# Scores of both head halves of four attention tiles in one group of matmuls, in a list-scheduled attention, GLU and tanh kernel

## The chip, the cores and the metric

The kernel runs on one core of a Trainium2 chip. The metric is the device time of one execution in microseconds (us). TensorE (PE in the views) multiplies, VectorE (DVE), ScalarE (ACT) and GpSimd (POOL) work on elements, and SyncE (SP) issues the transfers (DMAs). A matmul writes into one of eight banks of the accumulator memory PSUM, from which DVE and ACT read.

## The reference, cut to what matters

```python
# q, k, v: 2 batches x 8 heads x 768 tokens x 64; nb = 24 blocks of 32 tokens
k_sum = k.reshape(B, H, nb, 32, D).max(axis=3)
v_sum = v.reshape(B, H, nb, 32, D).mean(axis=3)
scores_l = q @ k^T / 8, only where |i - j| < 16, else -1e9
scores_s = q @ k_sum^T / 8 + log(32)
a = softmax(concat(scores_l, scores_s))
x = a @ concat(v, v_sum)                      # 1536 tokens x 512
xn = x / sqrt(mean(x * x) + 1e-6) * rms_g
x = (silu(xn @ w_gate) * (xn @ w_val)) @ w_out   # d_ff 1536
h = x @ w_in                                   # d_ff 2048
out = (h - tanh(h)) @ w_out2
```

## The kernel before

The attention is cut into 12 tiles of 128 tokens, and each tile into two halves of four heads: 24 units. `one_unit` (line 730) registers the operations of a unit. It loads queries, keys and values into a buffer `u` (line 741, by SP, one of three buffers), and for the later tiles POOL copies the summary keys into it (line 754). Then come eight instructions on PE, four matmuls of two passes each, that form the scores (line 786). They contract over 64 rows and go in turn to two PSUM banks, one for the even heads and one for the odd. DVE adds the mask and takes the maxima out of these banks (line 800, four), ACT takes the exponentials (line 814, four), PE transposes them (lines 834 and 839), ACT copies the transposes, PE multiplies with the values (line 877, and line 888 for the rest), and DVE and ACT scale. After both halves a tile is squared and summed (line 933), POOL takes a power (lines 923 and 924), and four transposes put the tile in columns (line 928).

Between the units stand products of the GLU. `step` takes one part of 128 columns of the hidden layer and a group of tokens. It forms the first products (lines 1046 to 1048, three matmuls for each product, since the numbers are split in a high and a low part) in a bank of the pool "mid", and later the second products in banks of the pool "bank". PSUM's eight banks are shared out as six of "bank", of which the running sums of the second products hold four and attention gets two, and two of "mid", which the first products use in turn. In the listings banks of the first pool are named bank_78 to bank_83 and those of the second mid_84 and mid_85. While the tiles 4 to 11 are worked through, PE alternates between units and steps. That stretch runs from 51 to 193 us. After it come the remaining GLU products, the wide stage and the second layer. Parts of the second layer's weights are made ahead by `make_out`: two loads (line 1607), three operations on DVE (lines 1614 and 1615), and a store (line 1617, `kd`).

The order on each engine is drawn up before the program is written. `Plan.order` is a greedy list scheduler: each operation has an engine, a duration, operations that it follows, slots (buffers or banks) that it occupies, and a latest start `late`. Of the ready operations an engine takes the one with the earliest latest start. `NUDGES` is a table whose entries shift the latest starts of a stretch of operations by random amounts, so that another table draws another order. `emit` writes the program in that order. Each engine then works through its list strictly in order, SP with its transfers too.

Of the kernel before, what the change touches and what calls it, by code (L numbers as in the profile page):

```python
# [24 lines left out]
NTILE = NT // P  # L25
# [24 lines left out]
SIDE = -0.6  # L50
LEAD = 2.0
GAP = 0.1
PACE = 2.0
FIRST = 24.0
WARM = 12
# [30 lines left out]
DONE = 28.0  # L86
# [13 lines left out]
CHAINS = 2  # L100
NUDGES = [
    (628070, 15, 135, 3.0, 0.03),
    (337371, 447, 567, 6.0, 0.1),
    (691236, 198, 248, 6.0, 0.3),
    (786176, 451, 501, 3.0, 0.1),
    (62758, 204, 254, 1.5, 0.3),
    (554383, 216, 236, 3.0, 0.3),
    (163346, 273, 293, 3.0, 0.1),
    (520442, 369, 419, 6.0, 0.03),
    (444721, 367, 487, 6.0, 0.03),  # L110
    (784034, 319, 339, 1.5, 0.3),
    (3849, 445, 565, 3.0, 0.1),
    (539265, 390, 440, 3.0, 0.03),
    (238481, 328, 448, 1.5, 0.1),
    (99185, 149, 269, 6.0, 0.1),
    (963478, 15, 35, 1.5, 0.1),
    (452397, 85, 105, 3.0, 0.3),
    (293650, 132, 152, 6.0, 0.1),
    (113861, 29, 49, 1.5, 0.03),
    (954728, 341, 361, 3.0, 0.1),  # L120
    (350925, 277, 397, 6.0, 0.03),
    (362785, 181, 201, 6.0, 0.3),
    (471079, 244, 264, 6.0, 0.03),
    (796911, 373, 493, 3.0, 0.3),
    (271606, 317, 437, 3.0, 0.1),
    (98501, 291, 411, 1.5, 0.1),
    (489872, 270, 390, 1.5, 0.03),
    (610784, 343, 463, 1.5, 0.1),
    (186195, 139, 159, 3.0, 0.03),
    (201734, 281, 401, 1.5, 0.1),  # L130
    (679656, 360, 480, 1.5, 0.1),
    (151638, 179, 299, 1.5, 0.3),
    (445821, 271, 321, 1.5, 0.03),
    (490284, 473, 493, 3.0, 0.03),
    (181965, 454, 574, 1.5, 0.1),
    (983193, 73, 193, 6.0, 0.1),
    (965923, 242, 292, 6.0, 0.3),
    (532099, 109, 159, 1.5, 0.1),
    (17171, 86, 206, 1.5, 0.3),
    (289692, 123, 173, 1.5, 0.3),  # L140
    (668941, 107, 157, 6.0, 0.03),
    (607916, 388, 438, 1.5, 0.1),
    (96143, 112, 132, 3.0, 0.3),
    (797718, 351, 471, 1.5, 0.03),
    (619643, 247, 297, 1.5, 0.3),
    (508929, 194, 314, 6.0, 0.03),
    (145032, 284, 334, 6.0, 0.03),
    (260735, 508, 558, 3.0, 0.3),
    (618205, 11, 31, 3.0, 0.03),
    (738483, 311, 331, 3.0, 0.3),  # L150
    (565716, 320, 440, 1.5, 0.03),
    (588188, 51, 101, 3.0, 0.1),
    (706373, 307, 357, 6.0, 0.03),
    (249976, 111, 231, 3.0, 0.3),
    (288783, 185, 235, 3.0, 0.3),
    (20454, 522, 542, 3.0, 0.03),
    (929727, 350, 370, 3.0, 0.1),
    (216610, 360, 380, 1.5, 0.1),
]
VDUE = 20.0  # L160
FRONT = 0.0
# [38 lines left out]


class Plan:
# [25 lines left out]
    def order(self, filler=None, gap=0.0):  # L228
# [29 lines left out]
        free, ready, events, out = {}, {}, [], []  # L258
# [34 lines left out]
        def can(o, now):  # L293
# [12 lines left out]
        while events:  # L306
            now = events.pop(0)
            while events and events[0] <= now + 1e-9:
                events.pop(0)
            for eng, queue in list(ready.items()):  # L310
                if free[eng] > now + 1e-9:
                    continue
                for i, (_, _, o) in enumerate(queue):
                    port = o.port if eng == o.eng else o.alts[eng][2]
                    if o.ready <= now + 1e-9 and not (port and (shared > now + 1e-9 or yields(o, eng, now))) and sooner(o, eng, now) and apart(o, eng, now) and can(o, now):
# [20 lines left out]
                if o.port:  # L336
                    shared = end
# [77 lines left out]
def kernel(  # L415
# [68 lines left out]
    apart = {}  # L484
    plan.pools["raw"] = Buffers([raw_r.tile[:, i * 1024:(i + 1) * 1024].bitcast(U32) for i in range(2)])
    for name, n, size, dtype in (("ih", 2, 1024, F32R), ("il", 2, 1024, F32R), ("oh", 3, 512, F32R), ("ol", 3, 512, F32R)):
# [3 lines left out]
        else:  # L490
            at = APART + base
# [27 lines left out]
    def pe(us, fn, *after, **kw):  # L519
        return plan.op("pe", us, fn, after, **kw)  # L520
# [884 lines left out]
    q = 2 * P  # L1405
# [9 lines left out]
    for a, b in (("fh", "h"), ("fl", "l")):  # L1415
        k = "hl".index(b)
# [751 lines left out]

    summaries(0)
    for i in range(2 * GROUPS[0][1]):  # L2170
        unit(i // 2, i % 2, math.inf, "att")
    for f in range(NF1):
        if f == 8:
            summaries(1, *early_users)
# [6 lines left out]
    for k in range(len(wseq)):  # L2181
        step(k, times[k])
    i0 = 2 * GROUPS[0][1]
    for i in range(i0, 2 * NTILE):
        a, z = begin + LEAD, at - DONE
        unit(i // 2, i % 2, a + (z - a) * (i + 1 - i0) / (2 * NTILE - i0))
    for i in range(SOON):
        make_out(i, at - 4.0 * (SOON - i))
    combine(at - 2.0)
# [166 lines left out]
```

## Time and profile before

| | |
|---|---|
| time, median of 3 runs | 618.66 us (617.62 to 620.13) |
| profiled execution, its own time | 618.95 us |
| its span, first to last instruction | 617.2 us |
| PE busy | 608.9 us, 99% of the span |
| DVE busy | 519.1 us, 84% |
| ACT busy | 411.1 us, 67% |
| POOL busy | 71.3 us, 12% |
| granted TensorE clock, mean over the span | 1.000 |

The span is what the views show. The 1.75 us by which the execution's time is longer lie outside it. A busy share counts an instruction from its start to its modelled end, and matmuls overlap: the one after begins before the last one's end. What a matmul costs is therefore read from the distance between two starts. In the timelines a row is a group of like instructions in sequence, with the start, the time to the last end, the engine, the line, the tiles written and read, and, in brackets, the idle time of the engine ahead of it and what ended that.

### The profile page before, as it was taken

How to read it: one execution, taken by the hardware profiler on the slowest of the kernel's cores; microseconds unless marked ns; L12 is line 12 of the kernel's file. 1: busy time of each engine (PE TensorE's matmuls, PEld its weight loads, DVE VectorE, ACT ScalarE, POOL GpSimd, SP SyncE). 2: the span in 40 equal slices, each digit the busy share in tenths (PEclk: the TensorE clock that was granted, in tenths of full speed). 3: DMA queues.
4: the chain of work that ended last, by engine and by line, in shares of the span. 5: the costliest groups of instructions: out<-in, count | busy, mean ns of one | idle time of the engine just before them, and what ended most of it. 6: DMA issues, size and time to landing. Idle time of an engine off the chain costs nothing.

```text
span 617.2 us, 10511 instructions
## 1 busy us (share of the span) xinstructions
PE 608.9 (99%) x3572; PEld 525.7 (85%) x3572; DVE 519.1 (84%) x1120; ACT 411.1 (67%) x836; POOL 71.3 (12%) x127
## 2 busy tenths in 40 slices
PE   9899999999999999999999999999999999999997
PEld 7798878788888888888888888889888888899997
DVE  6789978778789976789787997999996478988986
ACT  4995889997766644577676975776765455644441
POOL 3121232111101010221000000413100000000100
PEclk9999999999999999999999999999999999999999
DMA  8978667777600000253334255598769988599971
GB/s 313 338 272 315 229 206 236 264 265 256 199 1 0 36 1 1 81 191 119 116 106 137 72 201 206 203 342 307 284 200 314 366 295 296 195 420 419 418 288 69
DMA packets 47389, 132.41 MB, mean 215 GB/s; under 512 B 5560, under 2 KB 12136, under 8 KB 47336
## 3 DMA queue, kind: packets, MB, share of 16 engines
q1 hardware_dynamic: 47336, 131.74, 59.8%
q8 instruction: 28, 0.46, 0.3%
q14 instruction: 25, 0.20, 0.1%
HBM read 98.69 MB, written 33.03 MB: 213 GB/s over the span
## 4 chain that ended last, share of the span: by engine, by line
PE 82%; DMA 6%; DVE 5%; ACT 4%; SPq 2%; issue 1%; POOL 0%; DVEq 0%; ACTq 0%; POOLq 0%
PE bank L1047 15%; PE bank L1046 15%; PE bank L1048 15%; PE mid L1046 11%; PE mid L1047 10%; PE mid L1048 10%; DMA pad<-in_units_dram 2%; PE bank L877 2%; DMA wd<-in_units_dram 1%; PE bank L786 1%; PE bank L888 1%; DMA wd<-in_w_dram 1%; DVE wd L1006 1%; DMA hi<-in_w_dram 1%; DMA wd<-in_vsum_dram 1%
## 5 line engine op out<-in xcount | busy, mean ns | idle before, releaser
L1046 PE MATMUL mid<-hi,mix 128*128 128x512 f32 (+1 forms) x174 | 69.0, 396 | 0.0
L1048 PE MATMUL mid<-hi,mix 128*128 128x512 f32 (+1 forms) x174 | 64.3, 369 | 0.0
L1022 ACT CAST mix<-wd 128x512 fp32r<-128x512 f32 x66 | 40.6, 618 | 16.8 <-DVE wd L1006 8.8
L1046 PE MATMUL bank<-fours,mix 128*128 128x512 f32 (+1 forms) x128 | 49.2, 385 | 0.0
L1047 PE MATMUL bank<-fours,mix 128*128 128x512 f32 (+1 forms) x128 | 48.3, 377 | 0.0
L1048 PE MATMUL bank<-fours,mix 128*128 128x512 f32 (+1 forms) x128 | 48.2, 376 | 0.0
L1047 PE MATMUL mid<-lo,mix 128*128 128x512 f32 (+1 forms) x119 | 42.4, 356 | 0.0
L1024 DVE TENSOR_TENSOR mix<-wd,mix 128x512 fp32r<-128x512 f32 x59 | 40.5, 688 | 2.1 <-ACT mix L1022 1.9
L1046 PE MATMUL mid<-pad,mix 128*128 128x256 f32 (+1 forms) x124 | 41.4, 334 | 0.7 <-ACT lo L1890 0.7
L1047 PE MATMUL mid<-pad,mix 128*128 128x256 f32 (+1 forms) x124 | 41.2, 332 | 0.0
L1048 PE MATMUL mid<-pad,mix 128*128 128x256 f32 (+1 forms) x124 | 41.1, 332 | 0.0
L1318 DVE TENSOR_TENSOR lo<-lo,bank 128x512 f32<-128x512 f32 x36 | 24.7, 685 | 18.3 <-PE bank L1048 10.0
L1047 PE MATMUL bank<-pad,mix 128*128 128x512 f32 (+1 forms) x116 | 38.9, 336 | 0.0
L1046 PE MATMUL bank<-pad,mix 128*128 128x512 f32 (+1 forms) x116 | 38.9, 335 | 0.0
L1048 PE MATMUL bank<-pad,mix 128*128 128x512 f32 (+1 forms) x116 | 38.9, 335 | 0.0
L1046 PEld LDWEIGHTS mid<-hi,mix 128*128 128x128 f32 x174 | 32.8, 188 | 6.4 <-issue 2.3
L1048 PEld LDWEIGHTS mid<-hi,mix 128*128 128x128 f32 x174 | 32.7, 188 | 5.8
L1315 ACT COPY lo<-mid 128x512 f32<-128x512 f32 x36 | 20.8, 585 | 21.2 <-PE mid L1048 21.0
L814 ACT ACTIVATE pad<-pad,st 128x184 f32<-128x184 f32 x88 | 32.8, 442 | 2.7 <-DVE st L800 2.6
L800 DVE CUSTOM_DVE_ANT_0 pad<-bank,rest 128x184 f32<-128x184 f32 x88 | 25.5, 343 | 4.3 <-PE bank L786 3.9
L1046 PEld LDWEIGHTS bank<-fours,mix 128*128 128x128 f32 x128 | 24.1, 188 | 5.2 <-issue 1.1
L2050 DVE TENSOR_TENSOR wd<-wd 128x256 f32<-128x256 f32 x64 | 26.5, 424 | 1.7
(423 smaller groups left out, 1956.3 us busy)
## 6 DMA issues: line engine op xcount, KB each, us to landing
raw<-in_w_dram SPq DMA_DIRECT2D x38, 512.0 KB, 4.7
hi<-in_w_dram SPq DMA_DIRECT2D x16, 512.0 KB, 4.7
wd<-in_w_dram SPq DMA_DIRECT2D x14, 512.0 KB, 5.1
pad<-kv SPq DMA_DIRECT2D x8, 896.0 KB, 12.6
pad<-in_units_dram SPq DMA_DIRECT2D x16, 442.0 KB, 4.4
ki<-mix SPq DMA_DIRECT2D x12, 512.0 KB, 4.2
mix<-kv SPq DMA_DIRECT2D x6, 896.0 KB, 11.2
hi<-kv SPq DMA_DIRECT2D x6, 896.0 KB, 9.9
```

The lines of the kernel that those rows point to most:

```text
L786: nc.tensor.matmul(ps[e][:, j * SC:(j + 1) * SC], q[r, j], k[r, j, a:a + SC], start=(j == 0), stop=(j == NP - 1), skip_group_check=True,)
L800: nc.vector.tensor_tensor_reduce(sc[:, h * SC:(h + 1) * SC], ps[e][:, j * SC:(j + 1) * SC], mk[:, e * (SC - NB):e * (SC - NB) + SC], -1.0 ...
L814: nc.scalar.activation(s, s, AF.Exp, bias=st[:, 0, h:h + 1], scale=-1.0)
L877: nc.tensor.matmul(av[:, h * (D + 1):(h + 1) * (D + 1)], ph[:, h * P:(h + 1) * P], v[:, h], start=(h == 0), stop=False, skip_group_check=True,
L1022: a = act(0.52, lambda c=c: nc.scalar.copy(wh[:, c], d[:, c]), dep, chain.get(tag), slots=[wh])
L1024: on.tensor_tensor(wl[:, c], d[:, c], r32(wh[:, c]), ALU.subtract)
L1046: nc.tensor.matmul(o, ah, bh, start=first, stop=False, skip_group_check=True)
L1047: nc.tensor.matmul(o, ah, bl, start=False, stop=False, skip_group_check=True)
L1048: nc.tensor.matmul(o, al, bh, start=False, stop=last, skip_group_check=True)
L1315: return act(0.52, lambda: nc.scalar.copy(u[m][:], mx[m][:]), *after, *free, slots=[u[m], mx[m]])
L1318: return dve(0.62, lambda: nc.vector.tensor_tensor(u[m][:], u[m][:], my[m][:], ALU.add), *after, slots=[u[m], my[m]])
L2050: return pieces(0.35, lambda on: on.tensor_tensor(out(), x(), z(), op), *after)
```

## The change

The scores of the first and the second half of the tiles 8 to 11 become one operation on PE (16 instructions). The first half's go to two banks of "bank" as before, and the second half's to the two banks of "mid". For this `one_unit` becomes a generator that hands out its score function, the operations it follows and its slots, and takes back the operation that holds them. `claimed` makes an operation that wants a bank of "mid" stand back while such a joined group with an earlier latest start is ready but for its banks. The table `NUDGES` is replaced: of its 60 entries some stay, and there are now some 700.

```diff
+MORE = 0.62
+CLAIM = 0.0
+OVER = "mid", "bank"
+TWO = range(8, 12)
...
 NUDGES = [
     (628070, 15, 135, 3.0, 0.03),
-    (337371, 447, 567, 6.0, 0.1),
...
+    (387016, 216, 236, 3.0, 0.3),
...
+        self.claims = False
...
+        middle = self.pools["mid"]
+        over = [self.pools[k] for k in OVER]
+
+        def claimed(o, now):
+
+            return any(s.pool is middle and s.index is None for s in o.slots) and any(
+                q.claims and q is not o and q.late < o.late + CLAIM and q.ready <= now + 1e-9 and can(q, now, over) for _, _, q in ready["pe"]
+            )
+
+        def can(o, now, but=()):
             need = {}
             for s in o.slots:
-                if s.pool and s.index is None:
+                if s.pool and s.index is None and s.pool not in but:
...
-    def unit(*a):
+    def units_of(*args):
         n = len(plan.ops)
-        one_unit(*a)
+        parts = [one_unit(*a) for a in args]
+        wants = [next(u) for u in parts]
+        after = [o for w in wants for o in w[1]]
+        slots = [s for w in wants for s in w[2]]
+        p = pe(1.1 + MORE * (len(args) - 1), lambda: [w[0]((0, 1)) for w in wants], *after, slots=slots)
+        p.claims = len(args) > 1
+        for u in parts:
+            finish(u, p)
         unit_ops.extend(plan.ops[n:])
...
-        p = [pe(1.1, lambda: scores((0, 1)), *ks, load, slots=[u, *ps, sc, st])] * 2
+        both = yield scores, [*ks, load], [u, *ps, sc, st]
+        p = [both] * 2
...
+    a, z = begin + LEAD, at - DONE
+    for i in range(i0, 2 * NTILE, 2):
+        args = [((i + k) // 2, (i + k) % 2, a + (z - a) * (i + k + 1 - i0) / (2 * NTILE - i0), ("att", "mid")[k]) for k in range(2)]
+        if i // 2 in TWO:
+            units_of(*args)
+        else:
+            for t, hb, due, _ in args:
+                units_of((t, hb, due, "att"))
```

Line numbers of the changed kernel are higher by some 670: the scores are line 1458 there, the maxima 1472, the load of a unit 1413, the products 1719 to 1721, the weight loads 2280 and the stores 2290.

On PE, the score group of tile 10's first half stands alone before, between second products (written to bank_78 to bank_82 from `fours`, the hidden values):

```order
L1046 MATMUL bank_80<-fours,mix_67 128x256
L1047 MATMUL bank_80<-fours,mix_67 128x256
L1048 MATMUL bank_80<-fours,mix_67 128x256
L786 MATMUL bank_83<-pad_70 128x184
L786 MATMUL bank_79<-pad_70 128x184
L786 MATMUL bank_83<-pad_70 128x184
L786 MATMUL bank_79<-pad_70 128x184
L1046 MATMUL bank_82<-fours,mix_67 128x256
```

The changed kernel has there, for the same tile (a row is a matmul of two instructions):

```order
L1721 MATMUL bank_81<-fours,mix_67 128x256
L1458 MATMUL bank_79<-pad_70 128x184
L1458 MATMUL bank_83<-pad_70 128x184
L1458 MATMUL mid_85<-pad_70 128x184
L1458 MATMUL mid_84<-pad_70 128x184
...
L1719 MATMUL bank_78<-fours,mix_67 128x256
L1720 MATMUL bank_78<-fours,mix_67 128x256
L1721 MATMUL bank_78<-fours,mix_67 128x256
L1719 MATMUL mid_84<-hi_0_61,mix_67 128x256
```

The second half's scores moved up to the first half's, and into the banks of first products; three second products later a first product writes mid_84 again.

On DVE, before, the maxima of a half stand between the making of weights (L1614, L1615) and a step (L1116):

```order
L1615 SCALAR_TENSOR_TENSOR hi_0_62<-raw_68,hi_0_62 128x512
L800 ISA pad_70,st_88<-bank_79,rest_72 128x184
L800 ISA st_88 128x1
L800 ISA pad_70,st_88<-bank_79,rest_72 128x184
...
L800 ISA pad_70,st_88<-bank_83,rest_72 128x184
...
L1116 TENSOR_TENSOR th_92<-th_92,mid_85 128x256
```

In the changed kernel the eight maxima of tile 10 stand together, behind two operations that split weights (line 1697):

```order
L1697 TENSOR_TENSOR mix_67<-wd_0_74,mix_67 128x512 x2
L1472 ISA pad_70,st_89<-mid_84,rest_72 128x184
L1472 ISA st_89 128x1
L1472 ISA pad_70,st_89<-mid_84,rest_72 128x184
L1472 ISA st_89 128x1
L1472 ISA pad_70,st_88<-bank_83,rest_72 128x184
...
L1472 ISA pad_70,st_89<-mid_85,rest_72 128x184
```

DVE now reads mid_84 first, then bank_83 and mid_85, and bank_79 last.

On SP, before, the last two loads of units (`in_units_dram`) stand among the weight loads (`in_w_dram`) and the stores (`kd`) like this:

```order
L741 DMA pad_70<-in_units_dram 128x884
L1617 DMA kd_115<-hi_0_62 128x512
L1607 DMA hi_0_63<-in_w_dram 128x1024
L1617 DMA kd_116<-hi_0_62 128x512
L1607 DMA raw_68<-in_w_dram 128x1024
L741 DMA pad_70<-in_units_dram 128x884
L1617 DMA kd_117<-hi_0_62 128x512
```

In the changed kernel the last two loads, those of the second halves of the tiles 10 and 11, stand like this:

```order
L1413 DMA pad_70<-in_units_dram 128x884
L2290 DMA kd_115<-hi_0_62 128x512
L2280 DMA hi_0_63<-in_w_dram 128x1024
L2290 DMA kd_116<-hi_0_62 128x512
L2280 DMA raw_68<-in_w_dram 128x1024
L2290 DMA kd_118<-hi_0_62 128x512
L1413 DMA pad_70<-in_units_dram 128x884
```

The store of kd_118 moved ahead of the last load.

## Rows read from the trace of the kernel before

**Rows 1.** Windows: busy time (x instructions) by engine, granted clock, DMA share, GB/s
```profile
51.10:193.20 142.10, 141.18 (x867) 116.70 (x866) 119.38 (x313) 115.38 (x250) 25.93 (x64) 1.00 0.60 203
...
sum 617.20, PE 608.94 PEld 525.66 DVE 519.08 ACT 411.14 POOL 71.29; mean PE 152.24 PEld 131.41 DVE 129.77 ACT 102.79 POOL 17.82
```

**Rows 2.** Timeline of PE, second products in sequence
```profile
180.09 0.39 PE L1048 MATMUL bank<-fours,mix 128*128 128x512 f32 x1
180.32 0.39 PE L1046 MATMUL bank<-fours,mix 128*128 128x512 f32 x1
```

**Rows 3.** Timeline of PE, a score group between products
```profile
136.46 0.39 PE L1048 MATMUL bank<-fours,mix 128*128 128x512 f32 x1
136.78 0.89 PE L786 MATMUL bank<-pad 64*128 64x184 f32 x8
137.60 0.39 PE L1046 MATMUL mid<-hi,mix 128*128 128x256 f32 x1
137.83 0.28 PE L1047 MATMUL mid<-lo,mix 128*128 128x256 f32 x1
137.95 0.28 PE L1048 MATMUL mid<-hi,mix 128*128 128x256 f32 x1
```

**Rows 4.** Timeline of PE, values of a unit, transposes, the products after
```profile
144.64 1.00 PE L877 MATMUL bank<-pad 128*128 128x65 f32 x8
145.48 0.67 PE L888 MATMUL bank<-pad 113*128 113x130 f32 x4
145.98 0.60 PE L834 MATMUL bank<-ident,pad 128*128 128x128 f32 x4
146.34 0.36 PE L1046 MATMUL mid<-hi,mix 128*128 128x256 f32 x1
146.54 0.28 PE L1047 MATMUL mid<-lo,mix 128*128 128x256 f32 x1
```

**Rows 5.** Timeline of PE, a score group that waits inside
```profile
139.35 0.28 PE L1048 MATMUL mid<-hi,mix 128*128 128x256 f32 x1
140.28 1.52 PE L786 MATMUL bank<-pad 64*128 64x184 f32 x8 [0.66 <-POOL pad L754]
141.73 0.39 PE L1046 MATMUL mid<-hi,mix 128*128 128x256 f32 x1
```

**Rows 6.** Timeline of PE near the start, two score groups in sequence
```profile
12.34 1.72 PE L786 MATMUL bank<-wd 64*128 64x184 f32 x16 [0.20 <-DVE wd L672]
13.98 0.44 PE L834 MATMUL bank<-ident,pad 128*128 128x128 f32 x2
```

**Rows 7.** Timeline of DVE, first maxima after the group of rows 3
```profile
137.71 0.35 DVE L800 CUSTOM_DVE_ANT_0 pad<-bank,rest 128x184 f32<-128x184 f32 x1
...
137.98 0.34 DVE L800 CUSTOM_DVE_ANT_0 pad<-bank,rest 128x184 f32<-128x184 f32 x1
```

**Rows 8.** Timeline of PE, values of two units
```profile
119.94 0.33 PE L877 MATMUL bank<-pad 128*128 128x65 f32 x2
132.11 0.33 PE L877 MATMUL bank<-pad 128*128 128x65 f32 x2
```

**Rows 9.** Timeline of SP, loads of units, and one store behind a weight load
```profile
121.00 0.35 SPq L741 DMA_DIRECT2D pad<-in_units_dram  x1
...
131.98 1.54 SPq L741 DMA_DIRECT2D pad<-in_units_dram  x2
...
136.30 0.35 SPq L1607 DMA_DIRECT2D hi<-in_w_dram  x1
140.18 0.35 SPq L1617 DMA_DIRECT2D kd<-hi  x1
```

**Rows 10.** Timeline of POOL, summary keys copied into a unit
```profile
125.28 0.93 POOL L754 COPY pad<-rest 64x48 f32<-64x48 f32 x2 [1.73 <-DMA pad<-in_units_dram]
...
139.52 1.34 POOL L754 COPY pad<-rest 64x48 f32<-64x48 f32 x2 [0.59 <-DMA pad<-in_units_dram]
```

**Rows 11.** Timeline of PE, wide stage, a product that waits for a low part
```profile
385.38 0.39 PE L1046 MATMUL mid<-pad,mix 128*128 128x256 f32 x1 [0.66 <-ACT lo L1890]
```

More of the change, by code (lines that the diff above doesn't have):

```diff
@@ new lines @@
+    (420356, 98, 158, 10.0, 0.3),
+    (518851, 147, 162, 3.0, 0.1),
+    (962556, 92, 107, 10.0, 0.05),
+    (815842, 36, 51, 3.0, 0.1),
+    (205779, 72, 132, 6.0, 0.1),
+    (838670, 200, 215, 3.0, 0.1),
+    (700569, 54, 114, 3.0, 0.1),
+    (887637, 66, 126, 1.5, 0.3),
+    (169404, 246, 306, 10.0, 0.03),
+    (969633, 576, 636, 6.0, 0.1),
+    (737951, 343, 358, 10.0, 0.03),
+    (986652, 496, 526, 3.0, 0.03),
+    (209644, 129, 249, 6.0, 0.03),
+    (305303, 554, 614, 6.0, 0.3),
+    (466538, 262, 292, 6.0, 0.03),
@@ new lines @@
+    (352530, 536, 596, 1.5, 0.1),
+    (125217, 151, 271, 6.0, 0.03),
+    (239722, 90, 105, 1.5, 0.3),
+    (631405, 555, 570, 6.0, 0.3),
+    (3095, 388, 403, 3.0, 0.1),
+    (97424, 493, 508, 3.0, 0.1),
+    (819331, 573, 603, 3.0, 0.03),
+    (909281, 419, 479, 6.0, 0.3),
+    (986456, 542, 662, 1.5, 0.1),
+    (913223, 443, 458, 6.0, 0.03),
+    (13093, 419, 539, 10.0, 0.03),
+    (870073, 574, 694, 6.0, 0.1),
+    (81942, 382, 412, 1.5, 0.03),
+    (305193, 268, 298, 1.5, 0.1),
+    (200226, 376, 436, 3.0, 0.03),
@@ new lines @@
+    (301959, 160, 220, 10.0, 0.03),
+    (514194, 476, 536, 3.0, 0.3),
+    (87095, 405, 435, 3.0, 0.03),
+    (818786, 524, 554, 6.0, 0.3),
+    (633766, 326, 356, 3.0, 0.03),
+    (26065, 537, 597, 1.5, 0.1),
+    (905599, 588, 603, 6.0, 0.03),
+    (753852, 482, 512, 10.0, 0.03),
+    (34377, 402, 417, 6.0, 0.3),
+    (185313, 490, 550, 3.0, 0.1),
+    (925357, 285, 315, 1.5, 0.1),
+    (87926, 485, 605, 6.0, 0.1),
+    (192063, 152, 272, 1.5, 0.03),
+    (294987, 434, 554, 3.0, 0.3),
+    (539779, 99, 159, 6.0, 0.03),
@@ new lines @@
+    (2805, 186, 246, 3.0, 0.3),
+    (778727, 381, 396, 6.0, 0.03),
+    (445719, 142, 172, 1.5, 0.1),
+    (443475, 196, 316, 3.0, 0.1),
+    (832430, 266, 296, 10.0, 0.3),
+    (209133, 568, 628, 10.0, 0.1),
+    (203033, 266, 296, 3.0, 0.03),
+    (633564, 263, 293, 10.0, 0.1),
+    (684860, 358, 388, 3.0, 0.1),
+    (870298, 486, 546, 6.0, 0.03),
+    (603076, 515, 530, 3.0, 0.3),
+    (16971, 112, 127, 1.5, 0.1),
+    (49505, 571, 601, 1.5, 0.3),
+    (258900, 374, 494, 6.0, 0.03),
+    (618607, 96, 111, 1.5, 0.3),
@@ new lines @@
+    (875060, 398, 458, 6.0, 0.1),
+    (806965, 303, 423, 1.5, 0.03),
+    (468657, 464, 494, 6.0, 0.3),
+    (891033, 80, 95, 3.0, 0.1),
+    (487, 435, 555, 10.0, 0.1),
+    (27283, 559, 574, 6.0, 0.3),
+    (23993, 263, 323, 1.5, 0.03),
+    (127931, 597, 612, 10.0, 0.03),
+    (823600, 153, 213, 6.0, 0.03),
+    (758468, 283, 298, 1.5, 0.1),
+    (75663, 229, 244, 10.0, 0.1),
+    (506393, 547, 607, 6.0, 0.3),
+    (262599, 549, 609, 10.0, 0.1),
+    (917241, 523, 643, 10.0, 0.3),
+    (619638, 457, 472, 6.0, 0.3),
@@ new lines @@
+    (776860, 478, 493, 6.0, 0.3),
+    (278435, 279, 339, 1.5, 0.03),
+    (243773, 126, 141, 6.0, 0.03),
+    (934248, 365, 425, 10.0, 0.1),
+    (692173, 492, 552, 10.0, 0.3),
+    (818417, 127, 142, 6.0, 0.1),
+    (814854, 221, 236, 6.0, 0.3),
+    (181542, 589, 649, 1.5, 0.03),
+    (16627, 559, 574, 1.5, 0.3),
+    (551326, 145, 160, 6.0, 0.3),
+    (622024, 566, 686, 3.0, 0.3),
+    (513463, 560, 620, 3.0, 0.3),
+    (384188, 539, 599, 3.0, 0.3),
+    (432241, 598, 613, 3.0, 0.1),
+    (685011, 75, 105, 3.0, 0.03),
@@ new lines @@
+    (147736, 488, 518, 1.5, 0.1),
+    (498614, 587, 602, 10.0, 0.1),
+    (52220, 575, 590, 3.0, 0.1),
+    (497674, 534, 564, 1.5, 0.1),
+    (549373, 200, 230, 3.0, 0.1),
+    (469082, 131, 146, 1.5, 0.03),
+    (786147, 598, 658, 3.0, 0.1),
+    (620800, 330, 390, 1.5, 0.1),
+    (57191, 534, 654, 1.5, 0.1),
+    (61275, 533, 563, 1.5, 0.3),
+    (263151, 238, 298, 1.5, 0.03),
+    (576721, 281, 296, 1.5, 0.1),
+    (977953, 237, 297, 3.0, 0.03),
+    (885486, 515, 545, 3.0, 0.1),
+    (853680, 203, 218, 6.0, 0.3),
@@ new lines @@
+    (628204, 522, 552, 3.0, 0.03),
+    (635114, 75, 90, 1.5, 0.1),
+    (743792, 163, 193, 6.0, 0.1),
+    (81849, 570, 630, 1.5, 0.1),
+    (572413, 185, 200, 1.5, 0.03),
+    (363550, 54, 84, 3.0, 0.1),
+    (598543, 561, 681, 10.0, 0.3),
+    (972858, 96, 111, 1.5, 0.03),
+    (838709, 497, 557, 3.0, 0.3),
+    (668317, 597, 627, 10.0, 0.1),
+    (224980, 387, 507, 1.5, 0.03),
+    (353099, 500, 560, 6.0, 0.1),
+    (787582, 148, 178, 6.0, 0.1),
+    (866813, 343, 373, 1.5, 0.1),
+    (729873, 293, 323, 6.0, 0.1),
@@ new lines @@
+    (177437, 471, 531, 1.5, 0.1),
+    (781289, 245, 275, 3.0, 0.03),
+    (679342, 381, 411, 3.0, 0.03),
+    (250125, 344, 359, 1.5, 0.03),
+    (90065, 496, 556, 10.0, 0.1),
+    (483064, 440, 455, 1.5, 0.03),
+    (521773, 508, 568, 10.0, 0.03),
+    (399863, 152, 212, 6.0, 0.1),
+    (712524, 128, 248, 1.5, 0.1),
+    (346807, 553, 613, 10.0, 0.3),
+    (7781, 347, 377, 3.0, 0.3),
+    (850044, 44, 74, 1.5, 0.1),
+    (112503, 574, 589, 6.0, 0.3),
+    (457195, 518, 578, 6.0, 0.03),
+    (215469, 249, 309, 1.5, 0.3),
@@ L314, in order @@
                     port = o.port if eng == o.eng else o.alts[eng][2]
-                    if o.ready <= now + 1e-9 and not (port and (shared > now + 1e-9 or yields(o, eng, now))) and sooner(o, eng, now) and apart(o, eng, now) and can(o, now):
+                    if o.ready <= now + 1e-9 and not (port and (shared > now + 1e-9 or yields(o, eng, now))) and sooner(o, eng, now) and apart(o, eng, now) and can(o, now) and not claimed(o, now):
                         break
@@ L2170 @@
     for i in range(2 * GROUPS[0][1]):
-        unit(i // 2, i % 2, math.inf, "att")
+        units_of((i // 2, i % 2, math.inf, "att"))
     for f in range(NF1):
```

591 lines of the change are left out of this document (551 added, 40 removed).

## The prediction

> **What bounds the kernel now.** I read the windows first: between 51.1 and 193.2 us, the stretch in which units and steps alternate, PE is busy 141.18 of 142.10 us at a granted clock of 1.00 (2.4 GHz), and over the whole span 608.94 of 617.20 us [rows 1]. The reader is to see that no other engine comes near, so that time changes only by what PE issues or by what PE waits for. A busy share hides small waits, because each matmul's drain overlaps the next start. So I then read PE's timeline for prices. A product of 512 columns costs .227 us from start to start [rows 2], one of 256 columns .118 [rows 3]. A lone score group starts .32 after a 512 product instead of .227, lasts .82, and the 256 product behind it takes .23 instead of .118: .09 to enter, .82, .11 to leave, 1.02 in all [rows 3]. A unit's values cost .84 and .50, and four transposes .36 and .08 more of the product behind them, .11 each [rows 4].
>
> The order of the kernel before has in this stretch 339 products of 512, 84 of 256, 15 score groups, 130 transposes, and 16 blocks each of the two kinds of values. Priced, that is 77.0 + 9.9 + 15.3 + 14.4 + 13.4 + 8.0 = 138.0 us. The window is 142.1, so PE waits 4.1 us there. The largest wait is inside a score group: from 139.35 to 141.73 it is 2.38 us, where the product's .12, the entry's .09 and the group's .82 make 1.03. So 1.35 us is waiting, and it ends with POOL's copy of the summary keys [rows 5]. The other 2.75 us are small waits spread over the stretch.
>
> **The change part by part.** Outside the stretch the order changes little: up to 51 us PE's list is the same, and behind the stretch the same instructions priced in the new order give the same 417.4 us. That list holds the same matmuls in both kernels. I count the edits as follows.
>
> *The joining itself.* Four times two lone groups become one. Two groups in sequence took 13.98 − 12.34 = 1.64, which is twice .82 [rows 6], so inside nothing is saved. Saved is one entry and one exit for each pair, .09 + .11 = .20, and for four pairs **−.80**.
> The Trainium skill, TensorEngine Tiling (Array Packing), Key Properties, says that a change of tiling mode drains TensorE. If a drain were the whole overlap of a 512 product, .39 − .227 = .16 each way, four pairs would save 1.3 instead of .80, by an estimate from that rule. The trace agrees that the switch costs something, and its .09 and .11 decide how much.
>
> *The waiting group.* The order around 140.28 no longer exists: the tile there is joined, its second half's load goes out at another place. I take its **−1.35** as gone and price the waits of the new order by itself, below. Ends: −1.35 and 0.
>
> *Banks of first products.* A joined group holds both banks of "mid" until DVE has read them. Before, the first maximum starts at 137.71, .11 after the group's end at 137.60, and the next .27 later [rows 7]. The new DVE order reads mid_84 first, so mid_84 is free about .11 + .27 + .35 = .73 after the group, plus the time the semaphore takes, say .8. On tile 10, PE has only three second products of 256 and the exit to put in between, .36 + .11 = .47. PE waits about .3; the two splits of weights ahead of the maxima on DVE can make it later, so I take **+.4**, with ends .3 and .6. On the other three joined groups PE has at least .7 of other work behind the group and the exit, and I take nothing there, .3 each at worst. What queues behind the waiting product is PE's whole list, so these waits count in full.
> The Trainium skill, TensorEngine Tiling (Array Packing), Gotcha 1: PSUM Pressure, states that row tiles write to different banks. That speaks against the change: a joined group of two row tiles and two halves needs four banks at once. The trace agrees in that the matmuls of a group go to two banks in turn; no run here shows them in one. By it alone no time follows.
>
> *The second half's load.* It used to have the time of the first half's work to arrive; now the joined group needs it at once. A load goes out when the values of an earlier unit have freed the buffer. Two such chains can be read. Values at 119.94, load issued 121.00, keys copied by 125.28 + .93 = 126.21: 6.3 us [rows 8, 9, 10]. Values at 132.11, the second of two loads issued at 131.98 + 1.54 − .33 = 133.19, copied by 139.52 + 1.34 = 140.86: 8.75 us [rows 8, 9, 10]. In the new order PE's work from the values of tile 9's first half to the second half of tile 10's group is two blocks of values (2.68), two pairs of transposes (.44), 24 products of 256 (2.83), 3 of 512 (.68), the entry (.09) and the first half (.82): 7.54. Against 6.3 to 8.75 PE waits 0 to 1.2, and I take half of it, **+.6**. For tile 11 it is 2.68 + .22 + .44 + 12 × .227 + 9 × .118 + .91 = 8.04, a wait of 0 to .7, and I take **+.4**, a little over half, since this load stands in SP's list behind three stores. Tiles 8 and 9 have more work than 8.75 ahead of their second halves and wait for nothing. Moving these loads also moves the stores and weight loads around them; SP stood still at one of them for 3.5 us [rows 9] without a wait of PE for those weights, so they cost nothing unless a unit's load is stuck behind them (a rival).
>
> *Second products behind tile 11's group.* They need the low part of their hidden values, which DVE now makes behind four other operations. The nearest row is a product that waits .66 for a low part [rows 11]. Ends 0 and .66; by the order of DVE the part is ready about when the group ends, so I take the middle, **+.3**.
>
> *Four low parts that move from DVE to POOL, and the rest of the redrawn order.* POOL is busy 25.93 of 142.10 us in the stretch [rows 1] and has room. That takes work off DVE, which is not what PE waits for: nothing, unless one comes late, which is counted in the small waits. The other 2.75 us of small waits I carry over as they are: the new order has as many joints of the same kind. Their lower end, that they all go, is a rival below; a doubling is no likelier, and would give +2.75.
>
> **Sum.** −.80 − 1.35 + .4 + .6 + .4 + .3 = −.45. The profiled execution took 618.95, .29 above the median of 618.66; so 618.5 for it, and about **618.2** against the median.
>
> **The rivals.**
> *All waits go.* A new order that leaves no waits in the stretch gives −.80 − 4.1 = −4.9: 613.8. For it: the joined group takes the place of two points at which PE can be stopped, and much of the order was redrawn. Against it: two of the new joints have less work before them than the slow chain of a load needs.
> *The load sticks in SP.* Before, SP stood from 136.30 + .35 to 140.18, 3.5 us, behind a weight load, at a store that waited for DVE [rows 9]. In the new order three such stores stand between the last two unit loads, one more than before. If such a stop falls there, the chain is 1.06 (values to issue) + 3.5 + 6.33 (issue to POOL's copy, 133.19 to 139.52) + 1.34 = 12.2 against 8.04 of work: PE waits 4.2. With tile 10's full 1.2 that is −.80 − 1.35 + .4 + 1.2 + 4.2 + .3 = +3.95: 622.6. Waits for loads eat the gain (2.15 less .7 for the other waits) from 1.45 us on, and make the kernel slower by 0.5% from 4.5 on. Against it: a store can only stop SP that long when DVE is behind by as much, and DVE has gaps in the stretch (119.38 of 142.10 busy [rows 1]).
> *The joining joins nothing.* If the second half's keys come after the first half's scores in all four groups, PE stands between the halves, pays what the entry saved, and the 1.35 stays as a wait in another place: 0, or 618.7. For it: in the one group of rows 5 the stop lay in the middle, before the second half of a group's matmuls. Against it: tiles 8 and 9 have the time.
>
> **Chances.** A change under 0.5% (3.1 us) can't be told from none by a measurement of this kernel, whose three runs before lie .4% apart. The forecast .57, all waits gone .13, the stuck load .10, nothing joined .20. The forecast and the last give no measurable change, .77; the second gives faster, .13; the third slower, .10. The forecast's own range follows from its ends: at best 618.66 − 2.15 + .3 = 616.8, at worst (1.2 + .7 + .6 + .66 and .9 for the other three groups) 618.66 − 2.15 + 4.06 = 620.6. The range has to leave out no more than 2 in 10, so it reaches down to the case without waits, 613.8, and up to 621.0, short of the stuck load.
>
> **What would show it.** In the new profile: score groups of 16 instructions, 1.64 long, with one entry of .09 and one exit of .11 (the joining); for tile 10 the first product into mid .4 late, released by DVE's maxima (the banks); the groups of tiles 10 and 11 longer than 1.64 by .6 and .4, released by POOL's copy or the load (the loads); the second products behind tile 11's group .3 late, released by DVE (the low part); the first product of the wide stage about .5 earlier than 193.2, and from there the same distance to the end. The prediction is wrong if the last part, from there to the end, changes by more than 1 us, or if the small waits, carried over here, add up to something else than 2.75 by more than 2.

## The result, and the profile after

The changed kernel takes 623.08 us (median of 11 runs, 621.42 to 628.27), the kernel before 618.37 (11 runs, 617.08 to 620.63). The ratio is 1.0089, with a 95% interval of 1.0062 to 1.0116: slower, where 618.2 and no measurable change were forecast.

The profiled execution took 621.42 us, 2.5 more than that of before. Four of the 11 runs have a granted clock of 1.000 over the span (621.42 to 622.58); in the other seven it is .994 to .997, and they take 622.2 to 628.27. In the profiled execution the first 50 us, whose order on PE did not change, happened to be 1.4 us shorter than in that of before; behind them it is 3.7 us longer. So there are two things to find: these 3.7 us, which stand in the trace shown here, and the clock of other executions.

The windows of the changed kernel, against [rows 1]:

```profile
51.10:193.20 142.10, 137.32 (x857) 114.63 (x856) 118.28 (x303) 112.95 (x246) 32.92 (x68) 1.00 0.59 198
```

In the same 142.1 us PE is busy 137.32 instead of 141.18, and POOL 32.92 instead of 25.93. What PE waited for between 51 and 240 us (total, times, longest):

```profile
PE bank L1720 <- DVE fours L1740: 2.3, 2, 1.9
PE bank L1601 <- DVE st L1472: 2.0, 1, 2.0
PE mid L1719 <- DVE st L1472: 0.9, 2, 0.6
```

None of these waits is for a unit's load or POOL's copy of keys, and the 1.35 us of [rows 5] are gone. All end with DVE. PE's timeline shows where, behind the joined groups of the tiles 8 (at 112.49) and 11 (at 160.56). The two rows between them are the last second product behind tile 10's group and the first product into mid:

```profile
112.17 0.39 PE L1721 MATMUL bank<-fours,mix 128*128 128x512 f32 x1
112.49 0.89 PE L1458 MATMUL bank<-pad 64*128 64x184 f32 x8
113.22 0.79 PE L1458 MATMUL mid<-pad 64*128 64x184 f32 x8
113.94 0.50 PE L1719 MATMUL bank<-fours,mix 128*128 128x512 f32 x1
114.28 0.40 PE L1720 MATMUL bank<-fours,mix 128*128 128x512 f32 x1
114.52 0.40 PE L1721 MATMUL bank<-fours,mix 128*128 128x512 f32 x1
116.92 0.66 PE L1601 MATMUL bank<-ident,pad 128*128 128x128 f32 x4 [2.00 <-DVE st L1472]
...
147.04 0.28 PE L1721 MATMUL bank<-fours,mix 128*128 128x256 f32 x1
147.57 0.39 PE L1719 MATMUL mid<-hi,mix 128*128 128x256 f32 x1 [0.25 <-DVE st L1472]
...
160.56 0.89 PE L1458 MATMUL bank<-pad 64*128 64x184 f32 x8
161.28 0.79 PE L1458 MATMUL mid<-pad 64*128 64x184 f32 x8
162.00 0.50 PE L1719 MATMUL bank<-fours,mix 128*128 128x512 f32 x1
164.38 0.50 PE L1720 MATMUL bank<-fours,mix 128*128 128x512 f32 x1 [1.87 <-DVE fours L1740]
```

The joining works, and better than priced: 16 instructions take 162.00 − 160.56 = 1.44 us, not the 1.64 of [rows 6]; with one entry and one exit a pair saves .40 against two lone groups of 1.02. But behind the first group the four transposes of tile 7 (L1601) come 2.0 us late, and behind the last the second product comes 1.87 late. DVE at these places:

```profile
113.93 0.69 DVE L1697 TENSOR_TENSOR mix<-wd,mix 128x512 fp32r<-128x512 f32 x1 [0.43 <-ACT mix L1695]
114.54 1.78 DVE L1608 SCALAR_TENSOR_TENSOR pad<-pad,st 128x512 f32<-128x512 f32 x1
116.25 0.34 DVE L1472 CUSTOM_DVE_ANT_0 pad<-bank,rest 128x184 f32<-128x184 f32 x1
...
131.49 1.78 DVE L1608 SCALAR_TENSOR_TENSOR pad<-pad,st 128x512 f32<-128x512 f32 x1
...
149.65 0.75 DVE L1608 SCALAR_TENSOR_TENSOR pad<-pad,st 128x512 f32<-128x512 f32 x1
...
161.98 1.75 DVE L1608 SCALAR_TENSOR_TENSOR pad<-pad,st 128x512 f32<-128x512 f32 x1 [1.03 <-POOL st L1597]
163.65 0.68 DVE L1740 TENSOR_TENSOR fours<-th,fours 128x512 fp32r<-128x512 f32 x1
```

L1608 scales a tile (line 935 before) once POOL has made its power. Three times it takes 1.75 to 1.78 us instead of .75, and what PE waits for stands right behind it on DVE: the maxima, which free the banks, and the low part. On POOL one sees what else happens then (the row at 160.00 copies the last summary keys, those of tile 11's second half):

```profile
113.82 0.55 POOL L1597 TENSOR_TENSOR st<-st,mhalf 128x1 f32<-128x1 f32 x1
114.50 1.27 POOL L1740 TENSOR_TENSOR fours<-th,fours 128x512 fp32r<-128x512 f32 x1
...
130.83 0.55 POOL L1597 TENSOR_TENSOR st<-st,mhalf 128x1 f32<-128x1 f32 x1
131.41 1.30 POOL L1697 TENSOR_TENSOR mix<-wd,mix 128x512 fp32r<-128x512 f32 x1
...
160.00 1.03 POOL L1426 COPY pad<-rest 64x48 f32<-64x48 f32 x2 [7.62 <-DMA pad<-in_units_dram]
...
161.39 0.55 POOL L1597 TENSOR_TENSOR st<-st,mhalf 128x1 f32<-128x1 f32 x1
161.91 1.27 POOL L1697 TENSOR_TENSOR mix<-wd,mix 128x512 fp32r<-128x512 f32 x1
```

Each time a 512-wide operation stands behind the power in POOL's list and starts .04 to .08 us ahead of the scale that the same power releases; the scale ends .55 after POOL's operation does, so that most of its .75 runs when that is over. The planner keeps the two apart (`port` and `shared` in its code) and sets POOL's operation behind the scale, but on the chip nothing makes POOL wait for it. Tile 9's scale, at 149.65, has only copies of 48 columns behind its power, and takes .75.

The places of the loss follow from the starts of four PE instructions that are the same in both kernels by their number in PE's list (the 366th, the first one of the wide stage, the 1901st, the last):

| kernel | 366th | wide stage | 1901st | last | stretch | to 1901st | to the end |
|---|---|---|---|---|---|---|---|
| before | 50.89 | 193.24 | 344.95 | 613.78 | 142.35 | 151.71 | 268.83 |
| changed | 49.48 | 193.79 | 346.42 | 616.11 | 144.31 | 152.63 | 269.69 |

The front has the same order in both, and its 1.4 us are scatter between executions (the 366th starts at 49.7 to 51.0 in the kernels below). So the change costs 1.96 in the stretch and 1.78 behind it. The second part was not expected at all.

### The profile page after: what moved, and what is told of

It reads as the page before. It is cut to its first block, busy times and chain, and to the rows that moved or that the text cites. A ratio compares the mean times of both kernels' runs of the same rounds, so it can differ in the third digit from the quotient of the medians.

```text
span 619.6 us, 10500 instructions
## 1 busy us (share of the span) xinstructions
PE 607.7 (98%) x3572; PEld 525.4 (85%) x3572; DVE 522.0 (84%) x1113; ACT 410.3 (66%) x836; POOL 79.6 (13%) x134
## 4 chain that ended last, share of the span: by engine, by line
PE 81%; DVE 7%; ACT 5%; DMA 4%; issue 2%; POOL 1%; SPq 0%; ACTq 0%; POOLq 0%; DVEq 0%
PE bank L1720 14%; PE bank L1721 14%; PE bank L1719 14%; PE mid L1719 11%; PE mid L1721 11%; PE mid L1720 11%; DMA raw<-in_w_dram 3%; PE bank L1550 2%; PE bank L1561 1%; PE bank L1507 1%; PE bank L1458 1%; DVE pad L1608 1%; PE bank L1601 1%; ACT mix L1695 1%; DMA wd<-in_kt_dram 1%
## 5 line engine op out<-in xcount | busy, mean ns | idle before, releaser
L1697 DVE TENSOR_TENSOR mix<-wd,mix 128x512 fp32r<-128x512 f32 x57 | 39.8, 698 | 8.2 <-ACT mix L1695 7.9
L1720 PEld LDWEIGHTS bank<-fours,mix 128*128 128x128 f32 x128 | 24.1, 188 | 7.6 <-DVE fours L1740 3.6
L1719 PEld LDWEIGHTS bank<-fours,mix 128*128 128x128 f32 x128 | 24.1, 188 | 5.2 <-issue 0.6
```

The costliest lines, as they stand in the source:

```text
L1697: on.tensor_tensor(wl[:, c], d[:, c], r32(wh[:, c]), ALU.subtract)
L1719: nc.tensor.matmul(o, ah, bh, start=first, stop=False, skip_group_check=True)
L1720: nc.tensor.matmul(o, ah, bl, start=False, stop=False, skip_group_check=True)
```

## The experiments

Two theories stood against each other first. P: POOL's wide operation, begun just before DVE's scale, holds it up by 1.0 us, and PE pays. J: the joined groups hold all four banks until eight maxima are through, and the waits would be there anyway.

**e1_pool_waits.** The same order on every engine; three tiny copies keep POOL's wide operation behind the scale.

```diff
+            nr = ...; nr.first = lambda: nc.gpsimd.tensor_copy(tiny, flat()[:, 0:1])
...
+    for nr in [o for o in plan.out if isinstance(o, Op) and hasattr(o, "first") and o.start > 110]:
+        for o in plan.out:
+            if isinstance(o, Op) and o.eng == "pool" and o.us > 1.2 and nr.start < o.start < nr.start + 1.5:
+                o.fn = lambda first=nr.first, fn=o.fn: (first(), fn())
+                break
```

> The changed kernel, the same order on every engine, with one tiny POOL copy (128x1) that reads the scaled tile ahead of each of the three 512-wide POOL operations that stand right behind a tile's power (at 114.50, 131.41 and 161.91 us in the changed kernel's trace), so that they start after DVE's scale and not just before it. Theory P (POOL's wide operation, started first, holds up DVE's scale: 1.75 to 1.78 instead of .75 us, and PE waits for what stands behind it on DVE): the three scales take about .75, PE's waits of 2.0, .65 and 1.87 us shrink to about 1.0, 0 and .9, and the kernel is 2.8 us faster than the changed one, about 620.3. Theory J (the waits are those of the joined groups themselves, which hold all four banks until eight maxima are through): the waits stay within .3 each, and the time stays within 1 us of 623.1.

Measured: 620.54 us (6 runs, 619.26 to 622.38), 1.0041 of before (1.0028 to 1.0054), and a granted clock of 1.000 in all six. The scales and what follows them on DVE, POOL's wide operation at the first place, and what PE waited for:

```profile
115.77 0.75 DVE L1608 SCALAR_TENSOR_TENSOR pad<-pad,st 128x512 f32<-128x512 f32 x1
116.43 0.34 DVE L1472 CUSTOM_DVE_ANT_0 pad<-bank,rest 128x184 f32<-128x184 f32 x1
...
161.62 0.75 DVE L1608 SCALAR_TENSOR_TENSOR pad<-pad,st 128x512 f32<-128x512 f32 x1 [1.03 <-POOL st L1597]
162.29 0.69 DVE L1740 TENSOR_TENSOR fours<-th,fours 128x512 fp32r<-128x512 f32 x1
```

```profile
116.72 1.28 POOL L1740 TENSOR_TENSOR fours<-th,fours 128x512 fp32r<-128x512 f32 x1
```

```profile
PE bank L1720 <- DVE fours L1740: 1.3, 2, 0.9
PE bank L1601 <- DVE st L1472: 1.1, 1, 1.1
PE mid L1719 <- DVE st L1472: 0.2, 1, 0.2
```

The scales are back at .75, each long wait is about 1.0 shorter, and the stretch (50.60 to 192.47) takes 141.87 us: 2.44 less than in the changed kernel, .48 less than before. P holds for what the long scales added. J explains the 1.1 that is left behind tile 8's group; the .9 behind tile 11's is a low part behind a scale that itself waits 1.03 for the power. Against the four runs of the changed kernel at a clock of 1.000 (622.1) the gain is 1.6 us, the rest of the 2.5 between the medians is the clock. Behind the stretch e1 takes 422.8 us, no less than the changed kernel (422.3).

**e2_low_on_dve.** The four low parts alone go back to DVE.

```diff
-        kinds = {..., "pool": (GPC * (0.15 + 1.3 * us), lambda: rest(nc.gpsimd), True)}
+        kinds = {..., "pool": (GPC * (0.15 + 1.3 * us), lambda: rest(nc.vector), True)}
```

> The changed kernel, the same order, with the four low parts that had moved to POOL back on DVE at the places where they stand in the program; nothing else is moved. Theory P: only the scale near 114.5 us has a low part of these behind its power, so only that one returns to .75; the low part then stands on DVE ahead of the maxima with .68 us, and PE's wait there goes from 2.0 to about 1.7. The scales at 131 and 162 us stay at 1.75, and the time at 622 to 623. If the moving of these four were the cause by itself, the time would return to about 618.5 to 620.

Measured: 624.48 us (6 runs), 1.0096 (1.0075 to 1.0117), not to be told from the changed kernel; its two runs at a clock of 1.000 take 621.88 and 622.11. The scale at 115.54 is back at .75, those at 131.35 and 162.08 take 1.77 and 1.75 as in the changed kernel, and the wait for tile 7's transposes falls to 1.5. So it is not these four by themselves: two of the three wide operations that do the harm are splits of weights (L1697). The profiled run is one with a lower clock, and shows what that is. Windows around the wait at 162 to 164.5 (the column behind POOL's is the granted clock):

```profile
164.00:166.00 2.00, 1.51 (x8) 1.19 (x9) 2.00 (x14) 1.26 (x4) 0.00 (x0) 0.97 0.00 0
166.00:168.00 2.00, 2.00 (x7) 1.53 (x6) 1.62 (x8) 2.00 (x6) 0.00 (x0) 0.50 0.00 0
168.00:170.00 2.00, 2.00 (x9) 1.67 (x8) 0.00 (x0) 1.18 (x4) 0.00 (x0) 0.68 0.69 207
```

PE's timeline at the wait and in the slow part:

```profile
164.49 0.50 PE L1720 MATMUL bank<-fours,mix 128*128 128x512 f32 x1 [1.98 <-DVE fours L1740]
...
167.34 0.63 PE L1720 MATMUL mid<-lo,mix 128*128 128x512 f32 x1
167.77 0.63 PE L1721 MATMUL mid<-hi,mix 128*128 128x512 f32 x1
```

After the wait of 1.98 us PE runs on at 2.4 GHz for some 1.4 us, then at .50 of it, 1.2 GHz. By the windows' means (.97, .50, .68) that lasts 3.4 us, from 165.9 to 169.3. A 512 product costs .43 there instead of .23, and PE loses half of the 3.4 us, 1.7. The runs of e11, below, bear on whether the wait brings this on.

**e3_new_table_only** and **e4_join_only.** Each half of the change alone.

```diff
-TWO = range(8, 12)
+TWO = ()                      # e3: the new table, no joined group
...
 NUDGES = [                    # e4: joined groups, the table of before
```

> The changed program with the new table of nudges but no joined group (TWO is empty), so that an order is drawn anew that the joining has no part in. Its list has 512-wide POOL operations behind the power only of the first tile of the stretch and of the last. Theory P: no scale between 80 and 165 us takes over 1 us, and without those waits the time is 617 to 621. If any redrawn order costs as much (theory R), it is about 623, with waits of 1.5 us or more at other places.

> The changed program with the old table of 60 nudges: the last four tiles joined, the order otherwise drawn by the old table. Its list has a 512-wide POOL operation behind the power only of the first tile of the stretch. Theory P: no scale between 80 and 165 us takes over 1 us; what is left is the joining's own gain of .2 to .4 us for each pair and its waits for banks, up to .9 each: 617.5 to 621. Theory J: waits of about 2 us behind at least two of the joined groups, and 622 to 624.

Measured: e3 627.33 us (4 runs), 1.0152 (1.0138 to 1.0165); e4 624.53 (4 runs), 1.0109 (1.0095 to 1.0124). Neither came out where P had it. In both all scales between 80 and 165 us take under 1 us (.97 at most), so their waits have other causes. In e3 it is one wait of 3.9 us some 9 us into the wide stage (up to 205.74), and another for a copy of transposes:

```profile
PE mid L1719 <- ACT mix L1936: 3.9, 1, 3.9
PE bank L1550 <- ACT pad L1517: 1.2, 1, 1.2
```

Behind the first the clock falls too: by the windows it is .50 from about 206.3 to 209.8. This is theory R's picture rather than P's, a redrawn order that costs by waits at other places. In e4 the waits between 51 and 240 us sum to 4.8 us, of which the longest are these (e4 is another file; its L813 is the scores, L1074 a product). J had waits of about 2 us behind two groups, and they are not there either:

```profile
PE bank L813 <- DVE pad L933: 1.3, 1, 1.3
PE mid L1074 <- DVE st L827: 1.0, 1, 1.0
```

With the other program's table the time is 6.5 us (e4) and 9.3 us (e3) above before. These two runs tell nothing of the joining by itself, and the choice of them was poor: the table (57 entries before, 702 in the change) draws its shifts along the program's operations, so the same entries draw another order in another program, and the halves of such a change are not independent.

**e7_planted.** P from the other side: the kernel before with one useless wide POOL operation behind the power of the tiles 8 to 11.

```diff
-                nc.gpsimd.tensor_tensor(ss(), ss(), mhalf, ALU.pow)
+                nc.gpsimd.tensor_tensor(ss(), ss(), mhalf, ALU.pow); t < 8 or nc.gpsimd.tensor_tensor(spare[:, 0:512], spare[:, 0:512], spare[:, 512:1024], ALU.subtract)
```

> The kernel before, with one POOL operation more (128x512, on dead memory, its result unused) right behind the power of each of the tiles 8 to 11. PE, DVE, ACT and SP keep their order. Theory P: the four scales take 1.2 to 1.8 us instead of .75, with no joined group near. What of it reaches PE depends on what stands behind the scale on DVE: in this order the maxima for which PE's list waits stand elsewhere, so PE loses 0 to 1 us, 618 to 619.5. If a long scale always costs PE its length, 622. If the scales stay at .75, theory P is wrong about the cause of their length.

Measured: 619.76 us (12 runs), 1.0027 (1.0015 to 1.0040). DVE:

```profile
133.23 1.79 DVE L935 SCALAR_TENSOR_TENSOR pad<-pad,st 128x512 f32<-128x512 f32 x1
...
148.32 0.35 DVE L800 CUSTOM_DVE_ANT_0 pad<-bank,rest 128x184 f32<-128x184 f32 x1
148.86 1.22 DVE L935 SCALAR_TENSOR_TENSOR pad<-pad,st 128x512 f32<-128x512 f32 x1
```

POOL at the second place:

```profile
148.25 1.28 POOL L924 TENSOR_TENSOR keys<-keys 128x512 f32<-128x512 f32 x1
```

The scale takes 1.2 to 1.8 us (1.79, 1.22, 1.70 and 1.67) without any joined group, and PE loses 1.2 us in three waits for it ahead of the columns (L928), a little more than the 0 to 1 expected. The maxima, which read PSUM and one operand from SBUF, run beside POOL's operation at their .34. The Trainium skill, SBUF — State Buffer, SBUF: two separate sides, says that VectorE and GpSimd share one pair of ports under an exclusive lock, which an operation of GpSimd, or one of VectorE with two inputs in SBUF, holds for its whole length, while the other blocks. The trace agrees, with 1.79 against .75; no run here shows a port itself.

**e8_new_rest** and **e5_old_rest.** Theory B: behind the stretch it is the redrawn order that costs. From 190 us of the plan on, the operations outside attention get the latest starts that they have in the other kernel (e8: before with the new ones; e5: e1 with the old ones).

```diff
+LATES = {...}                 # by number of the operation
...
+        k = -1
+        for o in self.ops:
+            k += not hasattr(o, 'unit')
+            if not hasattr(o, 'unit') and k in LATES:
+                o.late = LATES[k]
```

> The kernel before (no joined groups), and from 190 us on the operations outside attention get the latest starts of the new table, so that PE's list from the wide stage on is that of the changed kernel but for its first rows. Theory B: the part from the wide stage to the end takes about 422.5 instead of 420.5 us, and the time is about 620. If the joined groups' stretch leaves something behind that costs the rest its 2 us, the time is that of before, 618.

> The kernel of e1 (joined groups, wide POOL operations wait for the scales), and from 190 us on the operations outside attention get the latest starts that the table of before gave them, so that PE's list from the wide stage on is that of before but for its first 150 rows. Theory B (what e1 has still over before lies behind the stretch, where the redrawn order makes PE wait more): the part from the wide stage's first product to the end takes 420.5 us as before and not 422.8, and the time is about 618.3, that of before. If the 2.3 us are not the order's but come with what happened before, the part stays at 422 or more and the time at 620.5.

Measured: e8 620.86 us (12 runs), 1.0038 (1.0019 to 1.0057), with 423.4 us from the wide stage (192.42) to the last instruction (615.85): B holds from this side, with some .9 more than expected. e5 621.82 (6 runs), 1.0057 (1.0041 to 1.0073): missed, with 424.1 us from the wide stage on and not 420.5. Its stretch takes 141.65, and from the 1901st instruction on it takes 268.73, as before. Between them, at the seam where the old order meets what the new one left, two new waits of 1.2 us came (at 202 and 219 us):

```profile
PE mid L1725 <- ACT fours L1743: 1.2, 1, 1.2
...
PE mid L1725 <- ACT mix L1942: 1.2, 1, 1.2
```

**e6_low_first.** e5 with the low part ahead of the scale behind tile 11's group.

```diff
+    plan.out.remove(nr[0])
+    plan.out.insert(plan.out.index(lo[0]) + 1, nr[0])
```

> The kernel of e5 with one pair of DVE operations exchanged: the low part for the second products behind tile 11's joined group goes ahead of the scale that waits for the tile's power. If PE's wait of .9 us there is one for that low part behind the scale, it goes, and the time is .9 below e5's: about 617.4, under before. If the wait is set by the low part's own input, it stays.

Measured: 621.49 us (6 runs), 1.0048 (1.0033 to 1.0064), .3 under e5, less than runs scatter. The wait for the low part has gone, and the one that comes next took its place, two products later:

```profile
162.16 0.40 PE L1727 MATMUL bank<-fours,mix 128*128 128x512 f32 x1
163.37 0.66 PE L1607 MATMUL bank<-ident,pad 128*128 128x128 f32 x4 [0.81 <-DVE st L1478]
```

The columns need a bank of attention, and the joined group holds them until the maxima are through: this wait is J's.

**e9_old_from_330** and **e10_low_earlier.** e9 is the changed kernel with e1's copies, e6's exchange, and the old latest starts from 330 us on, where the two PE lists are the same for 300 rows and there is no seam. e10 exchanges two more neighbours on DVE near 229 us, the low part and a split of weights ahead of it.

> The changed kernel with three edits: wide POOL operations wait for the scales (e1), the low part goes ahead of the scale behind tile 11's group (e6), and from 330 us on the operations outside attention get their latest starts of before, at a place where the two PE lists are the same for 300 rows, so that no seam is left. If the rest's loss is the redrawn order's, the part behind that place takes what it takes before (268.7 us for PE's last 1671 instructions, and not 269.7 as in the changed kernel), and with a stretch of 141.3 to 141.9 the time is 618.5, that of before (between 617.8 and 619.5). If a loss comes with the joined groups whatever the order, it stays at 620.5 or above.

> The kernel of e9 with two neighbours on DVE exchanged near 229 us: the low part, for which PE waits .45 us there, goes ahead of a split of weights that nothing waits for. The wait goes and the time is .5 us below e9's, 618.0, if no wait takes its place; e9's time, if the low part's input is as late.

Measured: e9 618.43 us (12 runs), ratio .9999 (.9985 to 1.0013); e10 617.67 (12 runs), .9987 (.9974 to 1.0000). Both as expected, e10 some .3 below, and e10 is at least as fast as before. In e9 the last 1671 instructions of PE (344.17 to 612.87) take 268.7 us, the 268.83 of before, and not 269.69. All that the change cost is found again by these edits, and the joined groups stay. In e10 the waits left between 51 and 240 us are those for banks:

```profile
PE bank L1601 <- DVE st L1472: 1.8, 2, 1.0
PE mid L1719 <- DVE st L1472: 0.2, 1, 0.2
```

**e11_two_of_three.** e1 without the third copy, so that PE's wait at 162 us is long again.

```diff
-hasattr(o, "first") and o.start > 110]
+hasattr(o, "first") and 110 < o.start < 150]
```

> The kernel of e1 without the third of its three waits: the wide POOL operation at 162 us starts before the scale again. The scale there takes 1.75 us and PE waits 1.9 us for the low part behind it instead of .9: 1.0 us longer than e1 by that, 621.5. If the long wait is also what lowers the granted clock behind it, some of the runs have a mean clock under .999, all of e1's had 1.000, and those runs are some 1.7 us longer again (the 7 matmuls behind the wait in e2's trace at half the clock), 623.2.

Measured: 622.67 us (6 runs), 1.0063 (1.0045 to 1.0081). The wait is long again:

```profile
PE bank L1720 <- DVE fours L1740: 2.4, 2, 2.0
```

Two runs have a clock of 1.000 and take 621.55 and 621.51; four have .997 and take 622.16 to 623.92. All six of e1, with a longest wait of 1.1 us in the stretch, have 1.000. So the long wait makes the lower clock more frequent; the 36 executions of e5, e6, e7 and e10, whose traces have no wait over 1.2 us, have .999 or more too. But it comes without one as well: of the executions of the kernel before, whose trace has no wait over 1.1 us, 2 of 56 have .997, and so have 2 of 4 of e4, whose trace has none over 1.3.

## Why the prediction was wrong

- **The step that failed first** is "four low parts that move from DVE to POOL, and the rest of the redrawn order", costed at nothing because POOL has room and DVE is not what PE waits for. I looked at POOL's busy share and not at what stands in its list behind the power. Three 512-wide operations there (only one of them one of the four low parts, the others splits of weights) made three scales 1.0 us longer, and at all three places what PE next had to wait for stood in DVE's list behind the scale. By e1 it cost the stretch 2.44 us. The same list before has such an operation next behind the power only at the first and the last of the tiles 4 to 11, and the scales there take .73 and .75.
- **The second** is that behind the stretch "the same instructions priced in the new order give the same 417.4 us". The prices were equal and the waits were not: 1.78 us more, past the 1 us that the prediction named as a sign of being wrong. e8 brings such a loss into the kernel before (2.9 us), and e9 takes it out from 330 us on, by the old order. About .9 lie before 345 us and .9 behind. One place is at 229 us, where PE waits .45 for a low part. By the trace a POOL operation of 256 columns (225.85, 1.07 long) runs beside a split on DVE that takes 1.22 us instead of .68 and stands ahead of that low part; no run takes the POOL operation away. e10's exchange of neighbours there takes the wait away and, with e9, ends at 617.67. The rest is spread over small places that I did not follow one by one, and its cause stays open.
- **The banks**: tile 10's wait of +.4 was right in place, kind and size: from 147.04 to 147.57 it is .53 from start to start, where a product of 256 takes .12 (the view's .25 counts from the modelled end). But to "take nothing there" on the other three joined groups failed. I had looked only for the next product in a bank of "mid"; the columns of an earlier tile need a bank of attention, which the group holds as well. That is 1.1 us behind tile 8's group in e1, and .81 behind tile 11's in e6.
- **The low part behind tile 11's group**: +.3 by order, 1.87 measured by the view; .9 of it stays when the scale is short (e1), since the scale itself waits for the power (1.03 idle).
- **The loads**: +.6 and +.4 were taken; no wait for a load or its keys is in the trace. The copies for tile 11's second half ended at 161.03, .25 ahead of its scores (161.28), so the margin was small but there.
- **The joining**: −.80 was taken, and .40 a pair, −1.6, measured. The term missed that a group's first and last steps are slow inside the .82 as well. The starts of single instructions in the traces, which the views merge, show it: in the group of [rows 3] they come in pairs, the second pair .26 behind the first, the others .16 apart, and the product behind .25 after the last pair. A joined group has .26, six times .16, and .25, so a pair of groups saves .20 there too. In [rows 6] the two groups took .70 and .95; that their sum is twice .82 was chance. The old wait of 1.35 is gone, as taken.
- **The clock** was in no step. In e2's trace its fall behind a wait near 2 us cost another 1.7 us. In the changed kernel 7 of 11 runs have a lower mean clock, and it is some 1 us of the median (623.08 against 622.1 for the runs at 1.000); where in those runs it fell was not traced.
- **The rivals**: that the load sticks in SP would have given 622.6, near the measured time, by a mechanism that did not occur; that closeness is chance. SP did stand still between the last two unit loads, from 147.54 to 151.96, at a store that waited for DVE. But the buffer for the last load came free only with the values at 153.34, the load went out 1.08 behind them (154.42), and PE waited for none of it.

The pieces: −.48 for the joining with its waits and the rest of the stretch, +2.44 for the scales, +1.78 behind the stretch, 3.74 together, and about +1 for the clock; measured 623.08 − 618.37 = 4.71. The first three are differences of single traces and add up to the traces' difference by construction. That the changed kernel's runs at a clock of 1.000 lie 3.7 above before is what bears them out.

## What to carry to other kernels

Where work moves to POOL, its busy share says little: look at which DVE operation with two operands in SBUF is released by POOL's own result, and at what stands next in POOL's list, since that starts first and holds DVE up for its whole length. A plan that knows of the lock does not help as long as nothing on the chip makes POOL wait. In a kernel in which PE is the bound, a redrawn order must be compared wait by wait to its end; equal work tells nothing of it, and a table that goes with one program is no baseline for another.

## What the runs showed of the hardware that was not expected

- Sixteen score instructions over four banks took 1.44 us, two lone groups of eight .82 each [rows 3]: pairs .16 apart, with a slow first step (.26) and a slow last one (.25) once for each group. Why these two steps are slow stays open.
- A DVE scale that starts .04 to .08 us behind a 1.27 to 1.30 us POOL operation takes 1.75 to 1.78 us instead of .75.
- In two traces the granted clock fell to .50 for about 3.4 us behind a long wait of PE: e2 (1.98 us) and e3 (3.9 us). In the traces of the changed kernel (2.00 and 1.87) and of e11 (2.0) it stayed at 1.00, though other executions of both have a mean of .997 or less (7 of 11, and 4 of 6). With waits up to 1.1 us in the stretch, as in e1, none of six has it; but 2 of 56 of the kernel before do, 2 of 4 of e4, and one of twelve each of e8 and e9. Why one execution has it and the next does not stays open.
